# Two head mixes of an attention block pair, moved into the four 64x64 quadrants of TensorE

## The chip, the cores and the metric

The kernel runs on one NeuronCore of one Trainium2 chip. Its engines are TensorE (PE: matrix products into PSUM; a separate instruction, shown as PEld, loads the stationary operand), VectorE (DVE), ScalarE (ACT), GpSimd (POOL) and SyncE (SP), whose queue issues every transfer between device memory and SBUF. Each engine works through its own instructions in program order and waits on semaphores where it needs another engine's result. The metric is the device time of one execution in microseconds. Before the change it was 1627.17 us, the median of three runs.

## The reference

Attention whose heads are mixed twice, followed by a gated two-layer product, all in float32. Eight batches, 12 heads, 448 positions, head size 64; the second part has width 768 and hidden width 1024.

```python
scores = scale * np.matmul(q, k.transpose(0, 1, 3, 2))       # 8 x 12 x 448 x 448
scores = np.einsum('bhij,hg->bgij', scores, w_pre)           # first head mix, 12 x 12
scores = scores - np.max(scores, axis=-1, keepdims=True)
attn = np.exp(scores)
attn = attn / (np.sum(attn, axis=-1, keepdims=True) + 1e-09)
attn = np.einsum('bhij,hg->bgij', attn, w_post)              # second head mix, 12 x 12
attn_out = np.matmul(attn, v)
a = x @ w1                                                   # x: attn_out as 3584 x 768
b = x @ w2
h = a * b @ w3
out = h @ w_out
```

## The kernel before, in words

The scores of a batch are computed head by head (`qk`, lines 196 and 197) and stored to device memory, so that they can be read back with another layout: rows of (position, head). A **block** is `IB` = 10 query positions of one batch with all 12 heads, that is 120 rows of 448 scores. A batch has `NB` = 45 blocks, the last of them 8 positions wide; there are 360 blocks in all.

For each block:

- `fetch` (line 212) reads the 120 rows from device memory, four blocks ahead of their use.
- `mix` (line 233) multiplies them by a 120x120 matrix that has `w_pre` ten times on its diagonal. The first `WHOLE` = 20 blocks do this in float32 as it stands (line 238). From then on the rows are split into two float32r parts by `split_r` (VectorE makes the high part on line 229, GpSimd the rest on line 230), and three products of 448 columns are summed (lines 241 to 243). The matrix is scaled by -0.125, so the largest score is the smallest entry.
- `largest` (line 249) takes each row's minimum on VectorE; `exp` (line 256) is the exponential on ScalarE, with the row's sum.
- `scale` makes one over the sum (lines 265 and 266) and multiplies the 120x120 matrix of `w_post` by it, row by row: on VectorE for the first `ACT_W` = 50 blocks (line 270), on ScalarE from then on (line 272).
- `post` (line 274) multiplies four pieces of 112 keys of the exponentials (the stationary operand) by that matrix (line 279). The result has keys on the partitions; line 285 copies it from PSUM to a tile `mt`, which collects `GB` = 15 blocks.

A float32 product appears in the profile as two passes of TensorE, a float32r one as a single pass. After 15 blocks, `av` multiplies `mt` by `v` for each pair of heads (line 310), in two column halves of 64. `qk_first` (line 160) computes the first batch's scores in float32 from two row halves of 64.

Between these steps TensorE works on the second part, called the background: first a folding of `w3` and `w_out` into one matrix (line 368), then the experts of batches 0 and 1 one by one (lines 530 and 561), then those of two batches at a time with seven products in place of eight (line 710). For the folding and the first experts, weights arrive as raw words and are converted in `to_f32` (lines 113 to 117), whose scratch tile `ca` lies in PSUM bank 5.

The order is written out by hand in `run`: one step per block. A step issues, in this order, its transfers, the conversions, the minimum of its block, the scaling of the block before, the next batch's scores, half of the background's share, the post-mix of two blocks earlier, the `av` work if any is due, the other half of the background, the pre-mix of the next block, the copies out of PSUM (`do_ends`) and, from block 20 on, the exponential. The planner `shares` spreads the background so that every step has the same number of passes, with costs of 2 for a piece of scores and 5.4 for an `av`. Copies and sums out of PSUM are held in lists (`ends`, `soon`, `later`) and issued at fixed places, or when `bank` wants a PSUM bank that is still to be emptied.

PSUM has eight banks. Banks 0 and 1 hold scores, 2 and 3 the pre-mix (by turns), 4 the post-mix, 5 the `av` sums and the converter's scratch, 6 and 7 the background. Once two batches are done at a time, the expert groups and the `av` sums take 5, 6 and 7 by turns (`next_bank`, line 599).

```python
for n in range(N + 6):
    ...
    if n < N:
        self.largest(n)
    ...
    if 0 <= n - 1 < N:
        self.scale(n - 1)
    ...
    advance(now // 2)
    if 0 <= n - 2 < N:
        self.post(n - 2)
    ...
    if n + 1 < N:
        self.mix(n + 1)
    self.do_ends()
```

## Time and profile before

| | |
|---|---|
| median of three runs | 1627.17 us (1625.48 to 1627.89) |
| profiled execution, first to last instruction | 1627.4 us |
| TensorE busy | 1579.8 us, 97% |
| ScalarE, VectorE, GpSimd busy | 1065.4, 1026.1, 1069.8 us |
| transfers | 436.48 MB, 268 GB/s on average |
| first block's minimum, last block's minimum | 23.7 us, 1436.3 us |
| granted TensorE clock | 0.990 of full speed |

The profile is of one execution, and it gives no time for that execution besides its span. A line of a group reads: line of the kernel, engine, operation, output and inputs by the program's names, shapes, count, then busy microseconds and mean nanoseconds of one, then the engine's idle time before them and what ended it. A line of the order in time reads: start, length, engine, line, operation, names, shape, count; consecutive instructions of one kind are merged into one line. On TensorE the lengths overlap, since a pass is shown until its last result is out: what one costs is read from one start to the next. `128*112 128x448` is a product with 128 rows and 112 columns of stationary operand, and 448 columns that move.

### The profile page before, as it was taken

The numbers are of one execution on the slowest core, as the hardware profiler recorded it, in microseconds if no ns is written. First come the engines' busy times: TensorE is split into PE (matmuls) and PEld (weight loads), VectorE is DVE, ScalarE is ACT, GpSimd is POOL, SyncE is SP. The second block draws the span as 40 slices with busy tenths as digits, with TensorE's granted clock in tenths as the row PEclk, the third lists the DMA queues.
The fourth block names the chain that finished last, engine by engine and source line by source line (L and its number), as shares of the span: only waits on it lengthen the run. The fifth ranks groups of instructions, "written<-read, shape, count | busy, mean of one in ns | idle before, by whom it ended". The sixth has DMA issues, their size and how long they took to land. (4 is left out here: it accounts for less than half of the span.)

```text
span 1627.4 us, 32069 instructions
## 1 busy us (share of the span) xinstructions
PE 1579.8 (97%) x10528; PEld 1416.6 (87%) x10528; DVE 1026.1 (63%) x2245; ACT 1065.4 (65%) x2554; POOL 1069.8 (66%) x904
## 2 busy tenths in 40 slices
PE   5999999999999999999999999999999999999999
PEld 2569998888899988988999899999999898999988
DVE  4868668778657877853465465655565567634573
ACT  3878768889867777776776676676775554542321
POOL 1347556667757877975577776877676666655774
PEclk7999999999999999999999999999999999999999
DMA  8989869999899999999988888889888766678875
GB/s 253 339 260 278 246 206 302 296 298 292 261 294 310 311 331 312 298 329 313 280 253 272 265 243 244 249 248 319 277 247 260 227 184 205 207 229 297 281 235 178
DMA packets 233906, 436.48 MB, mean 268 GB/s; under 512 B 21838, under 2 KB 159054, under 8 KB 233678
## 3 DMA queue, kind: packets, MB, share of 16 engines
q1 hardware_dynamic: 233742, 434.44, 84.6%
q8 instruction: 85, 1.39, 0.4%
q14 instruction: 79, 0.65, 0.1%
HBM read 300.27 MB, written 134.09 MB: 267 GB/s over the span
## 5 line engine op out<-in xcount | busy, mean ns | idle before, releaser
L230 POOL TENSOR_TENSOR rl<-r,rh 120x448 fp32r<-120x448 f32 (+1 forms) x340 | 422.9, 1244 | 275.5 <-DVE rh L229 79.8
L249 DVE TENSOR_REDUCE mn<-psm 120x1 f32<-120x448 f32 x360 | 223.9, 622 | 384.2 <-PE psm L243 373.6
L279 PEld LDWEIGHTS pso<-w,e 120*112 120x112 f32 (+1 forms) x2880 | 346.7, 177 | 35.8 <-ACT w L272 16.5
L279 PE MATMUL pso<-w,e 120*112 120x120 f32 (+1 forms) x2880 | 357.6, 267 | 10.9 <-ACT w L272 8.8
L285 ACT COPY mt<-pso 112x480 f32<-112x480 f32 x360 | 205.4, 571 | 199.4 <-PE pso L279 198.0
L710 PE MATMUL e<-eh,wu 128*128 128x448 f32 x1008 | 304.3, 371 | 0.6 <-DVE c L664 0.6
L256 ACT ACTIVATE e<-psm,mn 120x448 f32<-120x448 f32 x360 | 226.7, 630 | 17.8 <-DVE mn L249 17.6
L201 ACT COPY st<-psq 112x448 f32<-112x448 f32 x336 | 175.4, 533 | 56.9 <-PE psq L197 23.4
L229 DVE CAST rh<-r 120x448 fp32r<-120x448 f32 (+1 forms) x340 | 206.7, 608 | 2.5 <-DMA r<-raw_d 1.3
L710 PEld LDWEIGHTS e<-eh,wu 128*128 128x128 f32 x1008 | 187.2, 188 | 15.7 <-DVE c L664 1.4
L710 PE MATMUL e<-el,wu 128*128 128x448 f32 x504 | 187.6, 372 | 2.8 <-POOL el L649 2.8
L186 POOL TENSOR_TENSOR ql<-kq,qh 64x448 fp32r<-64x448 f32 x84 | 99.6, 1186 | 112.1 <-ACT qh L183 89.5
L310 PE MATMUL psa<-mt,v 112*64 112x150 f32 (+1 forms) x2304 | 158.5, 294 | 3.2 <-DMA v<-v 1.8
L310 PEld LDWEIGHTS psa<-mt,v 112*64 112x64 f32 x2304 | 145.1, 138 | 9.7 <-DMA v<-v 2.2
L664 DVE TENSOR_TENSOR c<-c,e 128x448 f32<-128x448 f32 x168 | 101.3, 616 | 67.4 <-PE e L710 62.6
L196 PE MATMUL psq<-kk,qh 128*112 128x448 f32 x336 | 126.0, 375 | 4.4 <-ACT st L201 4.3
L241 PE MATMUL psm<-rh,wph 120*120 120x448 f32 (+1 forms) x340 | 129.7, 381 | 0.0
L530 PE MATMUL eg<-xh,wu 128*128 128x448 f32 x384 | 127.3, 381 | 0.0
L272 ACT ACTIVATE w<-wpo,ri 120x120 f32<-120x120 f32 x310 | 123.0, 397 | 6.3 <-DVE ri L266 5.6
L243 PE MATMUL psm<-rl,wph 120*120 120x448 f32 (+1 forms) x340 | 124.2, 365 | 1.1 <-POOL rl L230 1.1
L242 PE MATMUL psm<-rh,wpl 120*120 120x448 f32 (+1 forms) x340 | 124.2, 365 | 0.0
L197 PE MATMUL psq<-kk,ql 128*112 128x448 f32 x336 | 123.1, 366 | 0.0
(116 smaller groups left out, 2996.6 us busy)
## 6 DMA issues: line engine op xcount, KB each, us to landing
r<-raw_d SPq DMA_DIRECT2D x352, 210.0 KB, 5.1
raw_d<-st SPq DMA_DIRECT2D x168, 392.0 KB, 4.9
wu<-w_d SPq DMA_DIRECT2D x104, 384.0 KB, 5.7
wu<-s_d SPq DMA_DIRECT2D x96, 384.0 KB, 4.3
v<-v SPq DMA_DIRECT2D x144, 224.0 KB, 4.4
wu<-w_d SPq DMA_DIRECT2D x51, 512.0 KB, 6.2
kq<-kq SPq DMA_DIRECT2D x42, 448.0 KB, 6.2
wu<-s_d SPq DMA_DIRECT2D x36, 512.0 KB, 4.4
```

What stands on the lines that cost most here:

```text
L196: nc.tensor.matmul(p, qh[:, cols], kk, start=True, stop=False)
L201: copy(st[:, c % 2], p)
L229: nc.vector.tensor_copy(rh[:K], r[:K])
L230: nc.gpsimd.tensor_tensor(rl[:K], r[:K], rh[:K].bitcast(F32), op=ALU.subtract)
L241: nc.tensor.matmul(p[:K, :S], self.wph[:K, :K], rh[:K], start=True, stop=False)
L249: nc.vector.tensor_reduce(mn[:K], p[:K, :S], axis=AX.X, op=ALU.min)
L256: nc.scalar.activation(e[:K], p[:K, :S], AF.Exp, bias=mn[:K], scale=-1.0, accum_out=sm[:K])
L279: nc.tensor.matmul(p[:, j, :, :w], e[:K, j * JT:(j + 1) * JT], w2[:K, :, :w], start=True, stop=True)
L285: self.ends.append((4, lambda: copy(dst, p[:, :, :, :w])))
L310: nc.tensor.matmul(self.psa[rows, g % 3, :W], v[:, j, rows], mt[:, j, 2 * g + s, :W], start=(j == 0), stop=(j == NJ - 1))
L530: nc.tensor.matmul(p, u[:, k % (K1 // 2), x], xs[y][:, k], start=(k == 0 and t == 0), stop=(k == K1 - 1 and t == 2))
L710: nc.tensor.matmul(p, w[:, k, x], ops[m, k][y], start=(k == 0 and t == 0), stop=(k == nk - 1 and t == 2))
```

## The change

Blocks are handled two at a time, 180 **sets** of two. A block's 10 positions are cut into two halves of `IH` = 5, so 60 rows (`HK`) of (position, head); one half is laid at partition 0, the other at partition 64 (`PP`). `fetch` reads both blocks of a set with two transfers, on even steps.

- **Pre-mix**: four float32 products, unsplit, one for each half (row quadrant, by `s`) and block (column quadrant, by `c`). A half's two blocks go to one PSUM bank, 2 or 3. The splits (`split_r`) and the three-part product are gone.
- **Minimum, exponential, scaling**: two instructions of each per set, one per half, on 128 partitions that hold both blocks. The scaling matrix has 60 columns instead of 120 and is always made on VectorE.
- **Post-mix**: for each half, seven pieces of 64 keys and each block, one float32 product with 60 moving columns: 28 per set. The block sets the row quadrant and the PSUM bank (4 or 5), the piece's parity sets the column quadrant. `put` copies one block per instruction to `mt`, which now has 128 partitions; `v` is padded to match.
- **Order**: an even step issues the minima at its start and the exponentials at its end; the odd step after it the scaling at its start, and at its end the post-mix followed directly by the next set's pre-mix. `av` goes ahead of the background, in odd steps only. The planner counts 8.6 passes for the mixes of an odd step.
- **Banks**: the experts take banks 6 and 7 by turns instead of 5, 6 and 7; the `av` sums share bank 2 with the pre-mix; the converter's scratch tile `a` lies in SBUF.

The diff, cut to its core (a line of "..." where lines are left out; the functions as they were stand above):

```diff
@@ -23,12 +23,15 @@
 KF, K1 = FF // 128, DM // 128
-WHOLE = 20
+IH = IB // 2
+HK = H * IH
+PP = 64
+JB = S // PP
+SETS = NB * B // 2
 FIRST = 48
 LATE = 2 * NB + GB + 2
-ACT_W = NB + 5
 PAIRS = ((0, 0), (0, 1), (1, 0))
@@ -109,7 +112,7 @@
-        a = self.bank(5, f"ca{name}").bitcast(I32)[:, :n]
+        a = self.cx.tile([128, CW], I32, tag="a", name=f"ca{name}", bufs=1)[:, :n]
         nc.vector.tensor_scalar(a, top, 3, 0x3FFFFFFF, op0=ALU.logical_shift_left, op1=ALU.bitwise_and)
@@ -209,80 +212,90 @@
     def width(self, n):
         return min(IB, S - n % NB * IB)
...
+    def fetch(self, m):
+        r = self.rp.tile([128, 2, S], F32, tag="r", name=f"r{m}", bufs=3)
+        self.rs[m] = r
+        b, t = divmod(2 * m, NB)
+        if t + 1 < NB and self.width(2 * m + 1) == IB:
+            src = self.raw_d[b][t * IB:(t + 2) * IB].rearrange("(c s i) h j -> s (i h) c j", c=2, s=2)
+            for s in range(2):
+                self.nc.sync.dma_start(r[s * PP:s * PP + HK], src[s])
+            return
+        for c in range(2):
+            b, t = divmod(2 * m + c, NB)
+            for s in range(2):
+                k = self.half(2 * m + c, s)
+                src = self.raw_d[b][t * IB + s * IH:t * IB + s * IH + k].rearrange("i h j -> (i h) j")
+                self.nc.sync.dma_start(r[s * PP:s * PP + H * k, c], src)
+
+    def half(self, n, s):
+        return min(IH, self.width(n) - s * IH)
+
+    def mix(self, m):
+        nc, r = self.nc, self.rs.pop(m)
+        ps = [self.bank(2 + s, f"psm{m}_{s}") for s in range(2)]
+        for c in range(2):
+            for s in range(2):
+                k = slice(s * PP, s * PP + H * self.half(2 * m + c, s))
+                nc.tensor.matmul(ps[s][c * PP:(c + 1) * PP, :S], self.wsc[k], r[k, c], start=True, stop=True)
+        self.psm[m] = ps
+
+    def largest(self, m):
+
+        nc, mns = self.nc, []
+        for s in range(2):
+            mn = self.ep.tile([128, 1], F32, tag="mn", name=f"mn{m}_{s}", bufs=4)
+            nc.vector.tensor_reduce(mn, self.psm[m][s][:, :S], axis=AX.X, op=ALU.min)
+            mns.append(mn)
+        self.mns[m] = mns
+
+    def exp(self, m):
+        nc, self.es[m] = self.nc, []
+        for s, (p, mn) in enumerate(zip(self.psm.pop(m), self.mns.pop(m))):
+            e = self.ep.tile([128, S], F32, tag="e", name=f"e{m}_{s}", bufs=4)
+            sm = self.ep.tile([128, 1], F32, tag="sm", name=f"sm{m}_{s}", bufs=4)
+            nc.scalar.activation(e, p[:, :S], AF.Exp, bias=mn, scale=-1.0, accum_out=sm)
+            self.es[m].append((e, sm))
+
+    def scale(self, m):
+        nc, self.w2s[m] = self.nc, []
+        for s, (e, sm) in enumerate(self.es[m]):
+            sa = self.ep.tile([128, 1], F32, tag="sa", name=f"sa{m}_{s}", bufs=2)
+            ri = self.ep.tile([128, 1], F32, tag="ri", name=f"ri{m}_{s}", bufs=2)
+            w2 = self.ep.tile([128, HK], F32, tag="w2", name=f"w2{m}_{s}", bufs=4)
+            nc.vector.tensor_scalar_add(sa, sm, 1e-9)
+            nc.vector.reciprocal(ri, sa)
+            nc.vector.tensor_scalar_mul(w2, self.wpo, ri)
+            self.w2s[m].append(w2)
+
+    def post(self, m):
+        nc, w2s = self.nc, self.w2s.pop(m)
+        if any(b in (4, 5) for b, _ in self.ends):
+            self.do_ends()
+        for s, ((e, _), w2) in enumerate(zip(self.es.pop(m), w2s)):
+            for j in range(JB):
+                a, z = divmod(j, 2)
+                at = (2 * a + s) * HK
+                for c in range(2):
+                    k = slice(c * PP, c * PP + HK)
+                    nc.tensor.matmul(self.pso[c][z * PP:(z + 1) * PP, at:at + HK], e[k, j * PP:(j + 1) * PP], w2[k],
+                                     start=True, stop=True)
+        for c in range(2):
+            n = 2 * m + c
+            w, (b, t) = self.width(n), divmod(n, NB)
+            a, u = divmod(t, GB)
+            if u == 0:
+                self.mt[b, a] = self.mp.tile([128, NJ, H, GB * IB], F32, tag="mt", name=f"mt{b}_{a}")
+            src = self.pso[c][:, :NJ * 2 * HK].rearrange("p (j s g i) -> p j s g i", j=NJ, s=2, g=H)
+            dst = self.mt[b, a][:, :, :, u * IB:u * IB + w]
+            self.ends.append((4 + c, lambda dst=dst, src=src, w=w: self.put(dst, src, w)))
+
+    def put(self, dst, src, w):
+        if w == IB:
+            self.nc.scalar.copy(dst.rearrange("p j g (s i) -> p j s g i", s=2), src)
         else:
...
+            for s, k in ((0, IH), (1, w - IH)):
+                self.nc.scalar.copy(dst[:, :, :, s * IH:s * IH + k], src[:, :, s, :, :k])
@@ -301,8 +314,7 @@
         if g % 3 == 0:
-            self.i_psa = self.next_bank() if self.pairs else 5
-            self.psa = self.bank(self.i_psa, f"psa{b}_{a}_{g}")[:, :3 * GB * IB].rearrange("p (g i) -> p g i", g=3)
+            self.psa = self.bank(2, f"psa{b}_{a}_{g}")[:, :3 * GB * IB].rearrange("p (g i) -> p g i", g=3)
         v, mt = self.vs.pop((b, a, g)), self.mt[b, a]
@@ -321,15 +333,15 @@
-            self.ends.append((self.i_psa, leave))
+            self.ends.append((2, leave))
         elif g % 3 == 2:
             q = self.psa[:, :, :W]
-            self.ends.append((5, lambda: nc.scalar.copy(h, q)))
-            self.soon.append((5, lambda: nc.vector.tensor_tensor(l, q, h.bitcast(F32), op=ALU.subtract)))
+            self.ends.append((2, lambda: nc.scalar.copy(h, q)))
+            self.soon.append((2, lambda: nc.vector.tensor_tensor(l, q, h.bitcast(F32), op=ALU.subtract)))
         self.later.append(self.load_v)
@@ -598,7 +610,7 @@
         self.n_groups += 1
-        return 5 + self.n_groups % 3
+        return 6 + self.n_groups % 2
@@ -784,10 +796,13 @@
         self.sz = self.sz.rearrange("p j g i -> p (j g i)")[:, :H * S].rearrange("p (h j) -> p h j", h=H)
-        w = self.kp.tile([128, S], F32R, tag="qh", name="wpre_s").bitcast(F32)[:GI, :GI]
-        self.wsc = cp.tile([GI, GI], F32, name="wsc")
+        w = self.kp.tile([128, S], F32R, tag="qh", name="wpre_s").bitcast(F32)[:, :PP]
+        self.wsc = cp.tile([128, PP], F32, name="wsc")
         nc.sync.dma_start(w, self.wpre)
-        self.wpo = cp.tile([GI, GI], F32, name="wpo")
+        self.wpo = cp.tile([128, HK], F32, name="wpo")
+        self.pso = [self.ps.tile([128, 512], F32, tag=f"b{4 + c}", name=f"pso{c}") for c in range(2)]
+        for p in self.pso:
+            nc.vector.memset(p[PP:, (NJ - 1) * 2 * HK:NJ * 2 * HK], 0.0)
         nc.sync.dma_start(self.wpo, self.wpost)
@@ -832,7 +843,8 @@
                 for g in range(HP):
-                    avs.setdefault(b * NB + (a + 1) * GB + (2 if g < 3 else 5), []).append((b, a, g))
+                    n = (b * NB + (a + 1) * GB + 2) | 1
+                    avs.setdefault(n if g < 3 else n + 2, []).append((b, a, g))
@@ -844,7 +856,7 @@
-            other = [len(qks.get(n, [])) * 2 + len(avs.get(n, [])) * 5.4 for n in range(first, last)]
+            other = [len(qks.get(n, [])) * 2 + len(avs.get(n, [])) * 5.4 + n % 2 * 8.6 for n in range(first, last)]
             level = (sum(other) + count) / (last - first)
@@ -882,18 +894,15 @@
         others(1)
-        for n in range(LF - 1):
-            self.fetch(n)
+        for m in range(LF // 2):
+            self.fetch(m)
         next(fold_pieces)
         next(fold_pieces)
-        self.split_r(0)
         self.mix(0)
-        self.fetch(LF - 1)
         others(2)
-        self.split_r(1)
@@ -936,8 +945,9 @@
                 next(setup, None)
-            if LF <= n + LF < N:
-                self.fetch(n + LF)
+            m, odd = divmod(n, 2)
+            if not odd and LF <= n + LF < N:
+                self.fetch(m + LF // 2)
             self.do_later()
@@ -957,16 +967,11 @@
                 self.split_kq(*x, nc.gpsimd, nc.gpsimd)
-            if n < N:
-                self.largest(n)
-            if n < WHOLE:
-                self.exp(n)
-
-
-            if 0 <= n - 1 < N:
-                self.scale(n - 1)
-            if n + 2 < N:
-                self.split_r(n + 2)
+            if m < SETS:
+                if odd:
+                    self.scale(m)
+                else:
+                    self.largest(m)
             self.do_soon()
@@ -993,22 +998,20 @@
+            for x in avs.get(n, []):
+                self.av(*x)
             advance(now // 2)
-            if 0 <= n - 2 < N:
-                self.post(n - 2)
+            self.do_ends()
             for x in firsts.get(n, [])[1:]:
                 self.later.append(self.qk_first(*x, (next(turn), next(turn))))
-            for x in avs.get(n, []):
-                self.av(*x)
             advance(now - now // 2)
-            if n + 1 < N:
-                self.mix(n + 1)
+            if odd and m < SETS:
+                self.post(m)
+                if m + 1 < SETS:
+                    self.mix(m + 1)
             self.do_ends()
-            while self.last:
-                self.last.pop()()
-
-            if WHOLE <= n < N:
-                self.exp(n)
+            if not odd and m < SETS:
+                self.exp(m)
             if third:
```

91 lines of the change are left out of this document (13 added, 78 removed).

## The prediction

> **What bounds the kernel now.** I read the page first, then the busy time by stage, then the head mixes in order of time on TensorE, then the other engines' groups.
>
> ```profile
> span 1627.4 us, 32069 instructions
> PE 1579.8 (97%) x10528; PEld 1416.6 (87%) x10528; DVE 1026.1 (63%) x2245; ACT 1065.4 (65%) x2554; POOL 1069.8 (66%) x904
> DMA  8989869999899999999988888889888766678875
> ```
>
> ```profile
> 24.00:248.00 224.00, 213.34 (x1318) 173.17 (x1317) 158.73 (x396) 164.41 (x383) 109.15 (x101) 0.96 0.86 269
> 248.00:753.00 505.00, 493.45 (x3526) 447.21 (x3525) 367.46 (x785) 396.40 (x969) 368.79 (x302) 1.00 0.93 304
> 753.00:1440.00 687.00, 679.41 (x4698) 625.28 (x4697) 396.66 (x914) 450.44 (x1099) 475.56 (x400) 1.00 0.81 248
> 1440.00:1627.40 187.40, 183.12 (x966) 166.94 (x964) 92.77 (x130) 47.42 (x94) 113.21 (x94) 1.00 0.77 252
> ```
>
> ```profile
> 24.00:248.00 224.00, 30.15 (x49) 34.96 (x96) 0.96 0.86 269
> 248.00:753.00 505.00, 85.59 (x138) 99.39 (x276) 1.00 0.93 304
> 753.00:1440.00 687.00, 107.81 (x173) 124.72 (x348) 1.00 0.81 248
> ```
>
> The second fence is busy time by stage (PE, weight loads, DVE, ACT, POOL, clock, DMA share, GB/s); the third is the same stages for the tile of row minima alone (DVE, ACT, then as before), so its DVE count is the number of blocks. TensorE is busy in 95 to 99% of the three stages with mixes while no other engine passes 79%. A microsecond taken from TensorE's own stream therefore shortens the span, until something else is late. The DMA share of 0.93 between 248 and 753 is the nearest other limit. The last 187.4 us hold expert work alone and the change does not touch them. Two blocks, the unit of the change, now take 2 x 505/138 = 7.32 us in the middle stage and 2 x 687/173 = 7.94 us in the long one. The span, 1627.4, and the median of the timed runs, 1627.17, differ by 0.2 us, so sums against the one stand for the other.
>
> **What a block's mixes cost TensorE now.** A stretch of the long stage, on PE in order of time (start, length, instruction):
>
> ```profile
> 900.62 0.98 PE L279 MATMUL pso<-w,e 120*112 120x120 f32 x8
> 901.37 0.45 PE L710 MATMUL e<-el,wu 128*128 128x448 f32 x1
> 901.65 0.56 PE L710 MATMUL e<-eh,wu 128*128 128x448 f32 x2
> ...
> 902.45 0.37 PE L241 MATMUL psm<-rh,wph 96*96 96x448 f32 x1
> ...
> 903.06 0.36 PE L196 MATMUL psq<-kk,qh 128*112 128x448 f32 x1
> ```
>
> Lengths overlap, so I go from start to start. A float32 product is two passes: four products of the post-mix stand as x8. From their start to the next pass's are 901.37 - 900.62 = 0.75 us, and the pass behind them holds TensorE 0.28 instead of the 0.20 that L241 to L196 show per pass ((903.06 - 902.45)/3), so 0.83. The pre-mix's three split passes take 0.61. One block: 1.44; two blocks: 2.88 us.
>
> **What it will cost: several tiles at once.** The trace has no product in a 64x64 tile, but products in half-array tiles, on the column side and on the row side:
>
> ```profile
> 866.50 0.98 PE L279 MATMUL pso<-w,e 120*112 120x120 f32 x8
> 867.41 3.28 PE L310 MATMUL psa<-mt,v 112*64 112x150 f32 x48
> 870.62 0.47 PE L241 MATMUL psm<-rh,wph 120*120 120x448 f32 x1
> 870.93 0.37 PE L242 MATMUL psm<-rh,wpl 120*120 120x448 f32 x1
> ```
>
> ```profile
> 39.97 0.92 PE L238 MATMUL psm<-r,wsc 120*120 120x448 f32 x2
> 40.82 1.01 PE L160 MATMUL psz<-kqz 64*112 64x448 f32 x4
> 41.76 0.44 PE L368 MATMUL psf<-fo,fw 128*128 128x384 f32 x1
> ```
>
> ```profile
> L279 PE MATMUL pso<-w,e 120*112 120x120 f32 (+1 forms) x2880 | 357.6, 267 | 10.9 <-ACT w L272 8.8 <-ACT mt L285 2.0
> ```
>
> Columns: 48 passes of 150 take 3.21 us, 0.067 each. The post-mix's spacing follows from its row of 0.98 and its pass of 267 ns (the group just above): seven spacings are 0.71, 0.102 each, 0.85 ns a column; its eight are 0.82. One at a time, 150 columns would take 0.128, so two run side by side. Rows: four passes of 448 take 0.94, while L238 takes 0.85 for two that cannot share. Again two at once. Nothing shows four at once; both splits together is what the change needs. I take four, because rows and columns each pair up fully, and keep two as the other bound.
>
> **Pass price in a tile.** A post-mix pass now moves 60 columns (0.051 us at 0.85 ns) against weights of 64. The weight loads give a second bound:
>
> ```profile
> L279 PEld LDWEIGHTS pso<-w,e 120*112 120x112 f32 (+1 forms) x2880 | 346.7, 177 | 35.8 <-ACT w L272 16.5 <-ACT mt L285 4.5 <-ACT e L256 1.3
> L310 PEld LDWEIGHTS psa<-mt,v 112*64 112x64 f32 x2304 | 145.1, 138 | 9.7 <-DMA v<-v 2.2 <-DVE cx L117 1.9 <-issue 0.6
> ```
>
> 48 weight columns less are 39 ns less, so 64 columns stream in about 64 x 0.81 = 52 ns. I take 0.053 a pass. Two blocks now have 2 x 7 x 2 = 28 products, 56 passes. Column tile 0 has j = 0, 2, 4, 6 of both sets, so the fuller tiles have 8 products: 16 passes, **0.85 us**. Pre-mix: four products of 448, one per tile, two passes of 0.38: **0.76**. **Changing the tiling:** post-mix before L310 lasts 0.91 instead of 0.82 (0.09), L310 lasts 3.21 where 24 pairs at 150 x 0.85 ns are 3.06 (0.15), the pass after takes 0.31 instead of 0.20 (0.11): **0.35** a visit. Post-mix and next pre-mix stand together, so one visit per two blocks. The sum is 1.96 against 2.88: 0.92 us less, times 180 is 166. The first 20 blocks now use the unsplit form, 0.85 instead of 0.61: 5 more. 1627 - 171 = **1456** with nothing waiting.
>
> A row of the trace has 0.067 us between starts in a row of passes; the change asks for one pass each 0.053/4 = 0.013. The Trainium skill (TensorE: Matmul & The Clock Gate, "Wait — 56ns, not 53.3ns?") says that start-to-start never goes below about 25 ns however narrow the product, and that instruction decode can cost about 62 ns a matmul. By 25 ns the post-mix would be 56 x 0.025 = 1.4 us, an estimate from that page, and the whole about 1555 before waits; no row here has passes dense enough to show such a floor.
>
> **The other engines.**
>
> ```profile
> L249 DVE TENSOR_REDUCE mn<-psm 120x1 f32<-120x448 f32 x360 | 223.9, 622 | 384.2 <-PE psm L243 373.6 <-PE psm L238 9.4
> L256 ACT ACTIVATE e<-psm,mn 120x448 f32<-120x448 f32 x360 | 226.7, 630 | 17.8 <-DVE mn L249 17.6
> L256 ACT ACTIVATION_READ_ACCUMULATOR e<-psm,mn 120x1 f32 x360 | 72.2, 201 | 0.0
> L285 ACT COPY mt<-pso 112x480 f32<-112x480 f32 x360 | 205.4, 571 | 199.4 <-PE pso L279 198.0
> L272 ACT ACTIVATE w<-wpo,ri 120x120 f32<-120x120 f32 x310 | 123.0, 397 | 6.3 <-DVE ri L266 5.6
> L265 DVE TENSOR_SCALAR sa<-sm 120x1 f32<-120x1 f32 x360 | 52.4, 146 | 23.0 <-ACT e L256 20.9
> L266 DVE RECIPROCAL ri<-sa 120x1 f32<-120x1 f32 x360 | 59.1, 164 | 12.3
> L270 DVE TENSOR_SCALAR w<-wpo,ri 120x120 f32<-120x120 f32 (+1 forms) x50 | 21.4, 429 | 1.7
> L229 DVE CAST rh<-r 120x448 fp32r<-120x448 f32 (+1 forms) x340 | 206.7, 608 | 2.5 <-DMA r<-raw_d 1.3 <-POOL wu L123 0.3 <-issue 0.3
> L230 POOL TENSOR_TENSOR rl<-r,rh 120x448 fp32r<-120x448 f32 (+1 forms) x340 | 422.9, 1244 | 275.5 <-DVE rh L229 79.8
> ```
>
> The splits disappear: DVE 207, POOL 423 us, both off the path. ACT loses 123 of scaling; DVE takes it for half as many columns, between 0 and 0.43 us, 0.25 taken: 78 more, under the 207. Minima, exponentials and copies out stay at 360, a few partitions taller at the same length. So no engine rises. Reads of raw scores stay at 360 transfers of the same rows; two per even step for two blocks, issued four blocks ahead as before. V tiles grow by 128/112. The memsets run once at the start, beside the 24 us before the first block.
>
> **The converted weights' scratch tile moves from PSUM to SBUF**, so three of its four VectorE operations read two SBUF tensors.
>
> ```profile
> L629 DVE TENSOR_TENSOR x<-t,x 128x448 f32<-128x448 f32 x18 | 20.4, 1144 | 0.0
> L664 DVE TENSOR_TENSOR c<-c,e 128x448 f32<-128x448 f32 x168 | 101.3, 616 | 67.4 <-PE e L710 62.6 <-issue 3.3 <-POOL c L691 0.7
> ```
>
> Two SBUF sources took 1.14 us, one PSUM source 0.62. That is 0 to 0.5 us on 72 x 3 operations; at the upper end 108 us of DVE, about what the casts return, so I take nothing. The Trainium skill (SBUF — State Buffer, "Who interferes with whom") says an instruction with two SBUF inputs contends with GpSimd reading SBUF. The two rows agree; with POOL losing 423 us the upper end is the less likely by that rule.
>
> **What is late next.** Before, two steps lay between a pre-mix and its post-mix; now it is one even step and the front of an odd one. With 0.92 off, two blocks last 6.40 us in the middle stage and 7.02 in the long one; less the 1.96 of mixes, 4.44 and 5.06 are left from the pre-mix's end to the post-mix's start. In them: the first minimum, 0.62. ACT has two copies out (1.14, begun when the post-mix ended 0.76 earlier, so done at 0.4) and the even step's share of its other work. Per two blocks ACT now has 2 x 396.4/138 = 5.74 in the middle stage; less 2 x 0.40 scaling, 1.66 exponentials and 1.14 copies, 2.14 are left, of which I put 60% into the even step: exponentials from 1.7 to 3.4. Two scalings of (0.15 + 0.16 + 0.25), the second behind the second exponential with 0.15 of handing over: 4.1. Long stage: 2 x 450.4/173 = 5.21, 1.61 left, 1.0 in the even step: 3.1, then 3.8. The second set's weights are wanted 0.43 after the start, at 4.87 and 5.49. It fits with 0.8 and 1.7 us spare. I charge misses: of 69 middle pairs a third late by 0.8 (18 us), of 86 long ones a tenth by 0.7 (6). Behind a late scaling stand post-mix, the next pre-mix and the next block's scores; behind that the next minimum. 1456 + 24 = **1480 us**.
>
> Edits with no charge: the expert groups on two banks instead of three (a group's nine passes last 1.8 us and its sum, 0.62, may be read out during the next; if DVE is more than 1.2 us late TensorE waits), and the attention-times-V sums sharing a pre-mix bank (three 16-pass groups there last 3.2 us, far longer than the copy that frees the bank; if the exponential is late, they wait with it).
>
> **Rivals.**
> - **The chain is the new wait (0.16).** If an ACT copy that waits for the even step's last expert group stands ahead of the exponentials, they start at 3.9 (even end 3.2, 0.2 to hand over, 0.53 copy): weights at 6.3, 1.4 us late in the middle stage, 1.0 in the long one. In half the pairs this is about 92 us: **1550**. For it: ACT is strictly ordered and the exponential is last in its step. Against: few groups leave by an ACT copy. In every pair it is 183: **1639**, slower (0.04).
> - **Short passes run two at a time, long ones four (0.09).** 28 x 0.053 = 1.48 instead of 0.85: 113 us more, and most waits vanish: **1575**. For it: the densest row has 0.067 between starts. Against: that row is full with two.
> - **Only two tiles at once (0.07).** Post-mix 1.48, pre-mix 1.52, switch 0.35 make 3.35 a pair, 0.47 over 2.88: 85 us, less 5 for the first blocks: **1707**, slower; it decides as soon as a pair's mixes pass 2.88. It is also the change not doing what it says.
> - **Transfers bind (0.07).** If 0.93 x 505 = 470 us of transfer time in the middle stage cannot shrink, 441 becomes 470: 1480 + 28 = **1508**. For it: the digits of 9 in the row of DMA shares. Against: TensorE is 98% busy there.
> - **No wait at all, and part of the 48 us in which PE is idle is saved too (0.05):** **1430**.
>
> **How the numbers follow.** Forecast 0.52: 1480, its own range 1445 to 1525. The range 1430 to 1590 takes in the first form of the chain, short passes by twos and the transfers, and leaves out the two slower cases and the edges, some 0.2. About 0.2%, or 3 us, is what this measurement tells from no change. Slower: 0.07 + 0.04 = 0.11; same 0.02 for a chain that eats just the gain; faster 0.87.
>
> **What would show it.** Right: post-mix and pre-mix rows of two blocks within 1.9 to 2.1 us from first start to the next other pass, with four starts of 64x64 passes some 10 ns apart; PE idle ahead of the post-mix under 40 us in all, with DVE's scaling named. Wrong: post-mix over 1.8 us a pair (tiles not side by side); PE waiting on the scaled weights for more than 90 us (chain); expert passes waiting on weight tiles in the middle stage (transfers); passes waiting on DVE sums (two banks).

## The result, and the profile after

The changed kernel takes **1585.53 us** (median of four, 1576.18 to 1591.93) beside 1626.82 for the kernel before on the same chip: a ratio of 0.9737, interval 0.9701 to 0.9774. It is faster, by 41 us; 147 were forecast. The time lies inside the stated range of 1430 to 1590 us, close to its upper end, with little more than a quarter of the gain that the sum gave. The page of the profiled execution begins:

```profile
span 1585.1 us, 45760 instructions
PE 1449.0 (91%) x18108; PEld 1144.7 (72%) x18108; DVE 978.4 (62%) x2215; ACT 990.2 (62%) x2252; POOL 653.4 (41%) x564
```

TensorE's busy time fell by 131 us (1579.8 to 1449.0), the span by 42. So the work went, and some 90 us came back as time in which TensorE stands.

A visit (post-mix and pre-mix of two blocks) in the long stage, on PE in order of time:

```profile
786.67 0.37 PE L722 MATMUL e<-eh,wu 128*128 128x448 f32 x1
786.97 1.09 PE L281 MATMUL pso<-w,e 60*64 60x60 f32 x54
787.85 0.59 PE L240 MATMUL psm<-r,wsc 60*64 60x448 f32 x2
787.89 0.22 PE L281 MATMUL pso<-w,e 60*64 60x60 f32 x2
787.95 0.92 PE L240 MATMUL psm<-r,wsc 60*64 60x448 f32 x6
788.80 0.46 PE L199 MATMUL psq<-kk,qh 128*112 128x448 f32 x1
789.10 0.37 PE L200 MATMUL psq<-kk,ql 128*112 128x448 f32 x1
```

From start to start the 56 passes of the post-mix take 787.85 - 786.97 = 0.88 us and the eight of the pre-mix 788.80 - 787.85 = 0.95. The pass ahead of the visit and the one behind it hold TensorE 0.30 each instead of 0.20. Together 0.88 + 0.95 + 0.10 + 0.10 = 2.03 us, where 1.96 was forecast. One pass each 0.88 / 56 = 0.0157 us is only possible with all four tiles at once: two at a time would need 28 x 0.053 = 1.48 by the prediction's price of a pass. The fuller tiles have 16 passes, 0.88 / 16 = 0.055 each, beside the 0.053 that the prediction took.

The stages after, cut at the row minima of blocks 0, 20, 50, 106, 120, 186, 270 and 358 (busy time by stage for the tile of row minima: stretch, length, DVE, ACT, granted clock, DMA share, GB/s); the rows of blocks 50 to 106 and 120 to 186:

```profile
248.10:460.00 211.90, 32.24 (x56) 37.51 (x112) 0.92 0.87 273
...
509.40:753.40 244.00, 38.06 (x67) 44.44 (x132) 0.99 0.99 331
```

The same cut through the kernel before and four of the experiments below gives the table (us). The forecast's column takes 0.92 off for each pair of blocks and 5 more off for the first twenty, whose unsplit pre-mix cost more before, and has no waits.

| blocks | before | forecast, no waits | after | E1 | E8 | E9 | E10 |
|---|---|---|---|---|---|---|---|
| 0-20 | 91.9 | 77.7 | 94.1 | 92.9 | 94.4 | 88.9 | 84.5 |
| 20-50 | 134.7 | 120.9 | 130.9 | 131.2 | 130.0 | 124.8 | 124.5 |
| 50-106 | 196.9 | 171.1 | 211.9 | 200.0 | 199.8 | 188.1 | 186.9 |
| 106-120 | 51.7 | 45.3 | 49.4 | 46.2 | 45.1 | 45.1 | 46.3 |
| 120-186 | 251.8 | 221.4 | 244.0 | 246.8 | 221.8 | 222.5 | 221.3 |
| 186-270 | 343.1 | 304.5 | 318.2 | 313.0 | 312.9 | 313.3 | 312.6 |
| 270-358 | 339.0 | 298.5 | 316.6 | 304.9 | 309.9 | 304.9 | 303.4 |

Three different things are seen. From block 186 on, 47 of 79 us came. In blocks 120 to 186 only 8 of 30 came, at a DMA share of 0.99. In the first 106 blocks nothing came: 436.9 us after against 423.5 before, where the forecast's column has 369.7, and blocks 50 to 106 alone became 15 us longer. There the granted clock is 0.92, against 1.00 in the same blocks of the kernel before (the first row; the second is blocks 120 to 186 of that kernel, whose DMA share was 0.96 already):

```profile
250.30:447.20 196.90, 34.76 (x56) 40.64 (x113) 1.00 0.92 291
...
498.90:750.70 251.80, 40.84 (x66) 46.80 (x131) 0.99 0.96 321
```

What TensorE waits for, in the whole changed kernel (us in total, times, longest):

```profile
PE pso L281 <- DVE sa L266: 52.3, 46, 4.3
PE pso L281 <- DVE w L268: 14.3, 31, 0.9
...
PE psa L322 <- DMA v<-v: 10.9, 8, 3.2
...
PE psa L322 <- ACT e L257: 7.4, 11, 1.5
...
PE psq L199 <- ACT st L204: 3.7, 1, 3.7
PE psm L240 <- DVE xl L344: 2.6, 12, 0.2
```

The post-mix waits 66.6 us for VectorE's scaling. The largest part, 27.9 us (25.8 and 2.1), lies between 248.1 and 460 us, in blocks 50 to 106; 15.2 (8.3 and 6.9) lie in blocks 186 to 358. How it comes about shows in two late visits. The first is of blocks 50 to 106 (VectorE's rows from the weight conversions to the first set's scaling, one of GpSimd, and the first exponential's sum):

```profile
310.52 1.16 POOL L190 TENSOR_TENSOR kk<-kq,kk 64x448 fp32r<-64x448 f32 x1
310.70 1.40 DVE L117 SCALAR_TENSOR_TENSOR ca<-cs,ca 128x384 int32<-128x384 int32 x1
...
311.71 0.20 ACT L257 ACTIVATION_READ_ACCUMULATOR e<-psm,mn 128x1 f32 x1
...
312.13 0.56 DVE L118 SCALAR_TENSOR_TENSOR ca<-cs,ca 128x384 int32<-128x384 int32 x1
...
312.83 0.56 DVE L120 SCALAR_TENSOR_TENSOR cx<-cm,ca 128x384 f32<-128x384 f32 x1
...
313.30 0.61 DVE L552 TENSOR_TENSOR em<-ea,eg 128x448 f32<-128x448 f32 x1
...
313.83 0.14 DVE L266 TENSOR_SCALAR sa<-sm 128x1 f32<-128x1 f32 x1
```

The sum is there at 311.91; VectorE is in a conversion, takes two more of its operations and one of the experts', and starts the scaling at 313.83, 1.9 us later. TensorE stands 2.53 us ahead of this post-mix. The second late visit is of the long stage (the timeline's rows of DVE and GpSimd, the sums of the exponentials, and the post-mix; reciprocals and the like left out):

```profile
1096.42 1.15 DVE L248 TENSOR_REDUCE mn<-psm 128x1 f32<-128x448 f32 x2 [4.91 <-PE psm L240]
...
1097.49 2.89 DVE L641 TENSOR_TENSOR t1o<-c,t1o 128x448 f32<-128x448 f32 x2
...
1099.22 0.20 ACT L257 ACTIVATION_READ_ACCUMULATOR e<-psm,mn 128x1 f32 x1
...
1099.83 0.21 ACT L257 ACTIVATION_READ_ACCUMULATOR e<-psm,mn 128x1 f32 x1
1100.30 0.61 DVE L676 TENSOR_TENSOR c1o<-c1o,e1o 128x448 f32<-128x448 f32 x1
1100.63 2.23 POOL L661 TENSOR_TENSOR el1o<-t1o,eh1o 128x448 fp32r<-128x448 f32 x2 [0.73 <-ACT eh1o L660]
1100.84 0.14 DVE L266 TENSOR_SCALAR sa<-sm 128x1 f32<-128x1 f32 x1
1101.21 0.61 DVE L268 TENSOR_SCALAR w<-wpo,ri 128x60 f32<-128x60 f32 x1
1101.97 0.68 PE L281 MATMUL pso<-w,e 60*64 60x60 f32 x28 [0.74 <-DVE sa L266]
1102.12 0.80 DVE L268 TENSOR_SCALAR w<-wpo,ri 128x60 f32<-128x60 f32 x1
1103.06 0.68 PE L281 MATMUL pso<-w,e 60*64 60x60 f32 x28 [0.41 <-DVE w L268]
```

The first exponential's sum is there at 1099.42 and the second's at 1100.04. VectorE is in the middle of two expert sums (L641) and takes one more (L676), so its scaling starts at 1100.84, 1.4 us after the first sum. Then the two scalings take 0.61 and 0.80 beside GpSimd's L661. TensorE stands 0.74 us ahead of the first set and 0.41 ahead of the second. From the pre-mix's end at 1096.42 the second exponential is done after 3.6 us and the second scaling after 6.5. Over all visits (worked out from the same rows, medians) it is 3.2 and 4.9; the forecast had 3.1 to 3.4 and 3.8 to 4.1. In the 54 visits in which TensorE stood ahead of the first pass it is 4.1 and 5.7, so there the exponentials are late too.

Two groups of the changed kernel that the forecast had priced:

```profile
L268 DVE TENSOR_SCALAR w<-wpo,ri 128x60 f32<-128x60 f32 x360 | 159.5, 443 | 12.6
L117 DVE SCALAR_TENSOR_TENSOR ca<-cs,ca 128x384 int32<-128x384 int32 x64 | 49.4, 772 | 2.2
```

The scaling's shortest, median and longest time in ns:

```profile
L268 DVE TENSOR_SCALAR w<-wpo,ri x360: 251/253/1334, 28.6 to 1392.3; 128x60 f32<-128x60 f32 x180
```

Taken at 0.25 us, it took that in the median, but 0.443 in the mean and up to 1.33. The mean is a mixture: the 199 scalings with no GpSimd operation beside them took 0.251 to 0.257 us, the 161 others 0.77 in the median (worked out from the rows of both engines). The conversion's L117 took 0.772 in the mean; before, the same operation stood at 0.562 (L114 of the kernel before, shown with the scratch experiment). It is a mixture too: 0.56 in the median with GpSimd idle, 1.37 beside a GpSimd operation.

### The profile page after: what moved, and what is told of

The parts are those of the page before. It is cut to its first block, busy times and chain, and to the rows that moved or that the text cites. A ratio compares the mean times of both kernels' runs of the same rounds, so it can differ in the third digit from the quotient of the medians.

```text
span 1585.1 us, 45760 instructions
## 1 busy us (share of the span) xinstructions
PE 1449.0 (91%) x18108; PEld 1144.7 (72%) x18108; DVE 978.4 (62%) x2215; ACT 990.2 (62%) x2252; POOL 653.4 (41%) x564
## 4 chain that ended last, share of the span: by engine, by line
PE 62%; DVE 16%; DMA 11%; ACT 7%; issue 3%; SPq 1%; POOL 0%; DVEq 0%; ACTq 0%; POOLq 0%
PE e L722 16%; PE psa L322 9%; PE pso L281 9%; PE psm L240 7%; DVE w L268 4%; DMA raw_d<-st 4%; PE psq L199 3%; PE e3o L722 3%; DMA v<-v 3%; PE e2o L722 3%; PE eg L542 3%; PE e1o L722 2%; PE psf L380 2%; ACT e L257 2%; PE psq L200 2%
## 5 line engine op out<-in xcount | busy, mean ns | idle before, releaser
L248 DVE TENSOR_REDUCE mn<-psm 128x1 f32<-128x448 f32 x360 | 207.6, 618 | 296.3 <-PE psm L240 295.9
L295 ACT COPY mt<-pso 128x480 f32<-128x480 f32 x352 | 198.0, 621 | 183.8 <-PE pso L281 183.3
L281 PEld LDWEIGHTS pso<-w,e 60*64 60x64 f32 x10080 | 199.7, 138 | 132.4 <-issue 32.5
L281 PE MATMUL pso<-w,e 60*64 60x60 f32 x10080 | 227.8, 228 | 73.3 <-DVE sa L266 52.3
L257 ACT ACTIVATE e<-psm,mn 128x448 f32<-128x448 f32 x360 | 226.0, 638 | 9.4 <-DVE mn L248 9.1
L240 PE MATMUL psm<-r,wsc 60*64 60x448 f32 (+1 forms) x1440 | 195.5, 580 | 11.3 <-DMA r<-raw_d 8.7
L322 PE MATMUL psa<-mt,v 128*64 128x150 f32 (+1 forms) x2304 | 160.4, 296 | 20.3 <-DMA v<-v 10.9
L322 PEld LDWEIGHTS psa<-mt,v 128*64 128x64 f32 x2304 | 147.2, 139 | 37.1 <-ACT e L257 18.0
L268 DVE TENSOR_SCALAR w<-wpo,ri 128x60 f32<-128x60 f32 x360 | 159.5, 443 | 12.6
L676 DVE TENSOR_TENSOR c<-c,e 128x448 f32<-128x448 f32 x168 | 101.3, 616 | 68.7 <-PE e L722 63.6
L661 POOL TENSOR_TENSOR el<-x,eh 128x448 fp32r<-128x448 f32 x90 | 105.9, 1195 | 72.5 <-ACT eh L660 48.0
```

Of the source, the lines that this page charges most:

```text
L240: nc.tensor.matmul(ps[s][c * PP:(c + 1) * PP, :S], self.wsc[k], r[k, c], start=True, stop=True)
L248: nc.vector.tensor_reduce(mn, self.psm[m][s][:, :S], axis=AX.X, op=ALU.min)
L257: nc.scalar.activation(e, p[:, :S], AF.Exp, bias=mn, scale=-1.0, accum_out=sm)
L268: nc.vector.tensor_scalar_mul(w2, self.wpo, ri)
L281: nc.tensor.matmul(self.pso[c][z * PP:(z + 1) * PP, at:at + HK], e[k, j * PP:(j + 1) * PP], w2[k], start=True, stop=True)
L295: self.nc.scalar.copy(dst.rearrange("p j g (s i) -> p j s g i", s=2), src)
```

## The experiments

Each run is named by its edit. E1, E2 and E3 start from the changed kernel, B1 and B2 from the kernel before, the others from an experiment. Times are medians; ratios are to the kernel before, run on the same chip.

### E1: the post-mix one set later

The theory is that late weights (the first rival, "the chain") hold the kernel: with one more set between pre-mix and post-mix, no weight can be late. The rival theory is that transfers hold it.

```
-                    n = (b * NB + (a + 1) * GB + 2) | 1
+                    n = b * NB + (a + 1) * GB
+                    n += 4 if n % 2 else 3
...
-            if odd and m < SETS:
-                self.post(m)
+            if odd:
+                if 0 < m <= SETS:
+                    self.post(m - 1)
```

> The changed kernel, but the post-mix of a set stands one set later (next to the pre-mix two sets ahead), with the attention-times-V work moved behind it. Nothing else differs. Theory CHAIN (the gain was eaten because minimum, exponential and scaling must fit between a pre-mix and the post-mix two steps on): in the trace after, TensorE stands 71 us ahead of post-mixes and 42 us inside them, and 88 us pass at half clock against 34 before, which costs up to 27 us. With 7 us more room all of that goes: 1586 - 113 - 27 = 1446 at the best, 1450 to 1480 expected. Rival TRANSFERS (transfers are 0.98 busy from 450 to 750 us): the middle stage stays at its 300 us and loses only what lies outside, 1475 to 1500. Rival BANKS or SCRATCH (two banks for experts, or the scratch tile in SBUF, took the gain): 1560 or more.

Measured: 1555.71 us (1552.07 to 1560.82), ratio 0.9561 (0.9529 to 0.9592). TensorE's group of the post-mix in E1 (busy and mean, then the idle time ahead of it):

```profile
L281 PE MATMUL pso<-w,e 60*64 60x60 f32 x10080 | 209.2, 225 | 0.0
```

and the waits of PE in E1:

```profile
PE psa L322 <- DMA v<-v: 21.4, 7, 5.6
PE psa L322 <- ACT e L257: 13.8, 13, 2.4
PE psq L199 <- ACT st L204: 12.9, 10, 4.1
...
PE psm L240 <- ACT e L257: 8.3, 7, 2.4
PE psm L240 <- DVE xl L344: 5.5, 12, 3.1
```

The idle time ahead of the post-mix is 0.0, so the lateness is gone entirely, and yet only 30 us came back. The five waits shown stand at 61.9 us where they were 24.6 in the changed kernel (with nothing for the pre-mix on the exponential): 37 of the 66.6 us moved to other places, and 66.6 - 37.3 = 29.3 is about what the span gained. The clock wasn't won back either: the expectation counted 88 us at half clock, and E1 has 94. The measured time meets none of the three expectations. The table says where it didn't help: blocks 120 to 186 (246.8 us) and 0 to 50.

### E2: exponential and scaling ahead of the even step's closing work

If VectorE's order alone makes the weights late, moving the scaling ahead of the closing copies and sums should help as much as E1.

```
-                if odd:
-                    self.scale(m)
-                else:
+                if not odd:
...
-            self.do_ends()
...
+                self.scale(m)
+            self.do_ends()
```

> The changed kernel, but exponential and scaling are both issued ahead of the copies and sums that end the even step; before, the exponentials came after them and the scaling at the start of the odd step, so VectorE reached it behind those sums. In the trace after, the second exponential is done 3.2 us after the pre-mix and the second scaling only at 4.9 (medians), and TensorE is ready at 4.5. Theory CHAIN with VectorE's order as the late link: scaling at about 3.2 + 1.0 = 4.2, most waits go: 1500 to 1535. If the exponential itself is the late link, nothing is gained: 1575 to 1590. If sums pushed behind the scaling then hold up the expert groups: slower than 1590.

Measured: 1581.0 us (1577.32 to 1591.7), ratio 0.9728 (0.968 to 0.9777), which is the changed kernel's. The closing copies and sums are not by themselves what makes the weights late. But the conversions, which an even step issues earlier, are still ahead of the scaling: in blocks 50 to 106 the post-mix of E2 waits 28.0 us for it (26.7 and 1.3), where the changed kernel has 27.9. Whether a scaling ahead of the conversions would be in time is not shown.

### B1: the kernel before with two expert banks

```
-            self.i_psa = self.next_bank() if self.pairs else 5
+            self.i_psa = 5
...
-        return 5 + self.n_groups % 3
+        return 6 + self.n_groups % 2
```

> The kernel before with one part of the change alone: in the last stage expert groups take banks 6 and 7 by turns, and the attention-times-V sums always bank 5. Theory CHAIN: the same within 0.3%, 1623 to 1632. Rival BANKS: the part that ate the gain, so 40 us or more: 1665 and up.

Measured: 1633.46 us, ratio 1.0032 (1.0018 to 1.0046). The third bank is worth some 5 us, so losing it is not the cause of a shortfall of 105.

### B2: the kernel before with the scratch tile in SBUF

```
-        a = self.bank(5, f"ca{name}").bitcast(I32)[:, :n]
+        a = self.cx.tile([128, CW], I32, tag="a", name=f"ca{name}", bufs=1)[:, :n]
```

> The kernel before with one part of the change alone: the converter's scratch tile lies in SBUF instead of PSUM bank 5. In the trace after, three of its operations take 0.66 to 0.77 us instead of 0.54, 42 us of VectorE in all. Theory CHAIN: off the path, the same within 0.3%, 1623 to 1632. Rival SCRATCH: the conversions set the first stage, so most of 42 us come out: 1645 to 1670.

Measured: 1675.89 us, ratio 1.0299 (1.0275 to 1.0324): 48 us slower. The groups by line and shape show the conversion's second operation, in the kernel before:

```profile
L114 DVE SCALAR_TENSOR_TENSOR ca<-cs,ca 128x384 int32<-128x384 int32 x64 | 36.0, 562 | 2.2
```

and in B2:

```profile
L114 DVE SCALAR_TENSOR_TENSOR ca<-cs,ca 128x384 int32<-128x384 int32 x64 | 71.2, 1112 | 2.2
```

Beside the GpSimd splits that the kernel before still has, the operation doubles. In the changed kernel, without the splits, it is 0.772. The Trainium skill (SBUF — State Buffer, "Who interferes with whom") says that a VectorE instruction with two SBUF inputs contends with a GpSimd instruction that reads SBUF; the three rows agree. So do the rows of the first late visit: 1.40 us at 310.70 beside GpSimd, 0.56 at 312.13 without.

### E3: the changed kernel with the scratch tile back in PSUM

Bank 0 is shared with the scores, since no bank is free.

```
-        a = self.cx.tile([128, CW], I32, tag="a", name=f"ca{name}", bufs=1)[:, :n]
+        a = self.bank(0, f"ca{name}").bitcast(I32)[:, :n]
...
-            for x in qks.get(n, []):
-                store = self.qk(*x, nq % 2, nc.scalar.copy)
+            for k, x in enumerate(qks.get(n, [])):
+                store = self.qk(*x, (k + 1 if fold_pieces or unit_pieces else nq) % 2, nc.scalar.copy)
```

> The changed kernel with the converter's scratch tile in PSUM again (bank 0; while weights are converted the scores' pieces start on bank 1). Theory SCRATCH (moving the tile alone cost 48 us in the kernel before, 13 in blocks 0 to 50 and 36 in 50 to 106): a good half of that comes back here, where GpSimd is less busy: 1545 to 1565, all of it in the first 106 blocks. If the cost in the kernel before came from GpSimd's splitting, which the change removes, nothing is gained: 1575 or more.

Measured: 1594.85 us, ratio 0.981 (0.9792 to 0.9828), nothing gained. Blocks 50 to 106 gained 7 us (211.9 to 204.7) and blocks 0 to 20 lost 14 (94.1 to 108.2) to the shared bank.

### E4: E1 and E3 together

The edit is the diffs of E1 and E3.

> The post-mix one set later (as e1_later_post) and the scratch tile in PSUM (as e3_scratch_psum). e1 alone gave 1556: its blocks 0 to 106 took 324 us, as the kernel before (324), though TensorE's own work there fell by some 45. Theory SCRATCH: that is what the first 106 blocks lack; 1510 to 1530. Theory TRANSFERS for the rest: blocks 120 to 186 stay at 240 us or more (247 in e1, 0.99 of the transfer time busy), where TensorE's own work asks for 222.

Measured: 1565.67 us, ratio 0.9633 (0.9614 to 0.9652), 10 more than E1. Its conversion is back at 0.562 us an operation, and blocks 50 to 106 gain only 5 us on E1 (194.8 against 200.0). As far as the shared bank lets it be read, the move to SBUF costs the changed kernel some 5 to 7 us and not B2's 48, so most of B2's price seems to have come from the splits that the change removes. The sharing hides some of it: in blocks 50 to 106 of E4 the scores wait 8.0 us (5.0 and 3.0) for VectorE. The 1510 to 1530 us expected were missed; blocks 120 to 186 stayed above 240, as expected.

### E5: the V tiles kept through a batch

The V tiles are loaded once a batch instead of once a group of blocks; from E4. They take six buffers instead of three, and the first ones are loaded earlier. This asks whether blocks 120 to 186 are held by transfers.

```
-        b, a, g = self.v_list.pop(0)
+        b, g = self.v_list.pop(0)
-        t = self.vp.tile([128, NJ, 128], F32, tag="v", name=f"v{b}_{a}_{g}")
+        t = self.vp.tile([128, NJ, 128], F32, tag="v", name=f"v{b}_{g}")
...
-        v, mt = self.vs.pop((b, a, g)), self.mt[b, a]
+        v, mt = self.vs[b, g], self.mt[b, a]
...
-        self.later.append(self.load_v)
+        if a == NG - 1:
+            self.later.append(self.load_v)
...
-        self.v_list = [(b, a, g) for b in range(B) for a in range(NG) for g in range(HP)]
+        self.v_list = [(b, g) for b in range(B) for g in range(HP)]
```

> As e4_both, but each v tile is loaded once per batch and kept for the three attention-times-V rounds instead of being loaded three times: 96 transfers of 256 KB fewer, 25 of 442 MB (to make room, one output tile of the folding and one work tile fewer). Theory TRANSFERS: blocks 120 to 186 lose 6 to 14 us against e4_both, and the waits on v (20 us in e1) go: 10 to 30 us less than e4_both in all. If transfers are hidden after all: within 5 us of e4_both.

Measured: 1550.85 us (1543.74 to 1553.92), ratio 0.9531 (0.9502 to 0.956). Blocks 120 to 186 went from 243.5 to 222.7 us, which is near the forecast's 221.4. So the V loads held that stage. Blocks 20 to 50 lost 12 us (135.4 to 147.3); why is not shown. E8 loads V otherwise there.

### E6: pre-mix and post-mix apart

Two visits for each pair instead of one, from E4: this prices the change of tiling.

```
+            if odd and m + 1 < SETS:
+                self.mix(m + 1)
...
-            if odd:
-                if 0 < m <= SETS:
-                    self.post(m - 1)
-                if m + 1 < SETS:
-                    self.mix(m + 1)
+            if odd and 0 < m <= SETS:
+                self.post(m - 1)
```

> As e4_both, but the pre-mix stands ahead of the second half of the background instead of right behind the post-mix, so TensorE changes its tiling twice as often. By the forecast's price of 0.35 us a visit: 180 x 0.35 = 63 us more than e4_both where nothing else limits, 40 to 65 with the stages that something else limits. If changing the tiling is nearly free: within 10 us of e4_both.

Measured: 1664.91 us, ratio 1.0244 (1.0225 to 1.0264), 99 more than E4, where 180 x 0.35 is 63. In blocks 270 to 358 it is 18.2 us on 44 pairs, 0.41 each, which is an upper bound: the pre-mix now waits there too, 7.6 us for ScalarE's copy of the `av` sums. The rest lies in the stages before, with new waits. Two mixes on their own, in that stage:

```profile
1303.00 0.37 PE L722 MATMUL e<-el,wu 128*128 128x448 f32 x1
1303.30 0.98 PE L240 MATMUL psm<-r,wsc 60*64 60x448 f32 x8
1304.21 0.67 PE L722 MATMUL e<-eh,wu 128*128 128x448 f32 x2
1304.72 0.36 PE L722 MATMUL e<-el,wu 128*128 128x448 f32 x1
1305.01 1.15 PE L281 MATMUL pso<-w,e 60*64 60x60 f32 x56
1306.09 0.67 PE L722 MATMUL e<-eh,wu 128*128 128x448 f32 x2
```

On entry the pass ahead holds TensorE 0.30 (0.10 more); on leaving the two passes at 1304.21 hold it 0.51 instead of 0.41. The pre-mix alone is 1304.21 - 1303.30 = 0.91 us, the post-mix alone 1306.09 - 1305.01 = 1.08. With 0.10 on either side of each, the two are 2.39, against 2.03 together: a visit more costs 0.36 us without any wait, which is the forecast's 0.35.

### E7: two of the four conversion operations left out

From E1; asks whether VectorE's conversions hold the first 106 blocks.

```
-        nc.vector.scalar_tensor_tensor(a, top, -0x40000000, a, op0=ALU.bitwise_and, op1=ALU.bitwise_or)
-        nc.vector.scalar_tensor_tensor(a, low, 29, a, op0=ALU.logical_shift_right, op1=ALU.bitwise_or)
```

> As e1_later_post, but two of the converter's four VectorE operations are left out (those that merge the exponent's top bit and the low bits, so the converted weights are wrong; 72 x 1.5 us, 108 us of VectorE by the trace after). Theory VECTOR: blocks 0 to 106 (324 us in e1 as in the kernel before, where TensorE's own work fell by 45) are held by VectorE's conversions and by the minima and exponentials that stand behind them: they fall to 285 to 300, the whole to 1520 to 1535. Rival TRANSFERS (0.82 to 0.92 busy there): the same within 8 us, 1548 or more.

Measured: 1535.91 us (1532.47 to 1536.87), ratio 0.9433 (0.9412 to 0.9454), 20 less than E1. By the cut of the table the first 106 blocks took 405.2 us where E1's took 424.1, 19 less; 369.7 is the forecast's. So the two operations are worth about a third of the 54 us by which E1 is over the forecast there.

### E8: V kept from the second batch on

From E1. From the second batch on V is loaded once a batch, into six buffers instead of three. To make room, the scratch tile shares the converter's output tile in SBUF, and the experts have one work tile fewer.

```
+        x = self.cx.tile([128, CW], F32, tag="x", name=f"cx{name}")[:, :n]
+        a = x.bitcast(I32)
...
-        t = self.vp.tile([128, NJ, 128], F32, tag="v", name=f"v{b}_{a}_{g}")
+        t = (self.vp2 if b and g > 2 else self.vp).tile([128, NJ, 128], F32, tag="v", name=f"v{b}_{a}_{g}")
...
-        v, mt = self.vs.pop((b, a, g)), self.mt[b, a]
+        v, mt = self.vs[b, 0 if b else a, g], self.mt[b, a]
...
-        self.later.append(self.load_v)
+        if b == 0 or a == NG - 1:
+            self.later.append(self.load_v)
```

> As e1_later_post, with v kept for the three rounds of a batch from batch 1 on (loaded once instead of three times), without e5's smaller buffers in the first stage and with the scratch tile in SBUF sharing the converter's output tile. Theory TRANSFERS for blocks 120 to 186 (247 us in e1, 223 in e5): they fall to 220 to 228 and nothing else moves: 1530 to 1540. If e5's gain came from elsewhere: 1550 or more.

Measured: **1534.18 us** (1530.57 to 1536.86), ratio 0.942 (0.9392 to 0.9448). It leaves nothing out and is 51 us under the changed kernel. Blocks 120 to 186 by the same cut, in E1:

```profile
493.70:740.50 246.80, 38.04 (x67) 44.55 (x132) 0.96 0.99 332
```

and in E8:

```profile
492.00:713.80 221.80, 38.00 (x66) 44.59 (x132) 1.00 1.01 341
```

The stage is 25 us shorter with fewer bytes to move, at a share that is still at its top. It meets the forecast's 221.4. In E1 the passes that use V wait 19.1 us for it in this stage, in E8 not at all. E1's bytes there, 332 GB/s x 246.8 us = 81.9 MB, would take 240 us even at E8's 341 GB/s, an estimate from the two rows; that the V buffers also let loads start earlier is not separated from it. Blocks 270 to 358 became 5 us longer.

### E9: E8 with the two conversion operations left out

The edit is E7's on E8. It asks whether the causes add up.

> The kernel that keeps v (e8) with two of the four VectorE operations of each weight conversion left out, as in e7, so the converted weights are not the reference's. It asks whether the causes found so far add up, and what is left of the forecast behind them. If they are independent (late weights, transfers of v, conversions on VectorE): 1534 - 20 = 1514 us, with blocks 0 to 106 at about 405 us (e8: 422, e7: 405) and blocks 120 to 186 at 222. If the conversions' 20 us only uncover the transfers or ScalarE in the first 106 blocks, it is the same 20 there and no more than that, and 370 us (the forecast's price for these blocks) stays out of reach by 35. If they overlap with the transfers of v: 1525 or more.

Measured: 1516.14 us (1510.15 to 1520.71), ratio 0.9325 (0.9296 to 0.9353): 18 less than E8. They add up to 2 us. Blocks 0 to 106 took 401.8 us (E8: 424.2) and blocks 120 to 186 took 222.5. To the forecast's 369.7 for the first 106 blocks 32 us are missing, about the expectation's 35.

### E10: E9 with half of the packed weights' transfers left out

```
+        last = None
...
-                words.append(self.words(jobs[n + 2][0], f"{self.n_words}"))
-                self.n_words += 1
+                src = jobs[n + 2][0]
+                if n % 2 == 0 or last[0] != src.shape:
+                    last = src.shape, self.words(src, f"{self.n_words}")
+                    self.n_words += 1
+                words.append(last[1])
```

> As e9, and every second job of the conversions works on the tile of the job before it and loads none of its own, so half of the packed weights' transfers (some 35 of 384 KB, about 13 MB in the first 106 blocks) are left out; the converted weights are wrong. If transfers hold the first 106 blocks behind the conversions (their share there is 0.88 to 0.95): 15 to 25 us less than e9 in these blocks, about 1490 to 1500 us in all. If what is left there is ScalarE's order (scores' copies and exponentials) or the narrow products' own waits: within 5 us of e9.

Measured: 1504.29 us (1499.31 to 1506.74), ratio 0.9239 (0.921 to 0.9267), 12 less than E9, between the two expectations. Of the profiled difference of 8.3 us, 4.4 lie in the first twenty blocks and 1.5 in blocks 20 to 106. So transfers held a little at the very start and hardly anything behind it, as far as two single executions tell: E9's four lie 10.6 us apart. What TensorE waits for here between 24 and 430 us:

```profile
PE psq L201 <- ACT st L206: 9.6, 9, 4.1
PE psm L242 <- ACT e L259: 5.3, 3, 2.4
PE psa L324 <- ACT e L259: 4.8, 6, 1.5
```

19.7 us of waits on ScalarE's copies of scores and its exponentials are left there. Blocks 20 to 106 are 19.4 us over the forecast's column, and 12.4 of these waits (3.0, 5.3 and 4.1) lie in them. No run took them away, so that cause is argued and stays open.

## Why the prediction was right or wrong

**Right: what the mixes cost.** The visit was put at 1.96 us and is 2.03: post-mix 0.88 (0.85), pre-mix and tiling changes 1.15 (0.76 and 0.35). The 0.35 for the change of tiling is 0.36 by E6's rows. All of this is 180 x 0.07 = 13 us of the shortfall. The two rivals about tiles that don't run four at once, 1575 and 1707 us, are out by the row of 56 passes in 0.88 us. So is the floor of 25 ns that the Trainium skill (TensorE: Matmul & The Clock Gate, "Wait — 56ns, not 53.3ns?") states: the passes of four tiles start 15.7 ns apart. Within one tile they start 0.055 us apart, so a floor for a single tile is not ruled out.

**Right: the long stages, once two waits are gone.** For blocks 120 to 358 the forecast's column has 824.4 us, and E8 takes 844.6. Of the 20 us over it, 119 pairs x 0.07 = 8 are the visit's; the rest is other waits. The forecast's 24 us for late weights would fill the gap as well, but in E8 no weights are late, so that match would be luck.

**Right: no charge for two banks (near enough).** 5 us by B1, where nothing was charged.

**Wrong: the term "what is late next", 24 us.** It is 66.6 us of TensorE standing ahead of the post-mix, between the two signs set for it (under 40 for right, over 90 for the chain). What was mis-sized is the way from the exponential to the scaled weights. The working counted ScalarE's other work (2.14 us a pair in the middle stage) but none of VectorE's; it had 0.15 us of handing over and 0.25 for a scaling. The runs show VectorE still in conversions or in expert sums, 1.9 and 1.4 us late in the two visits shown, and a scaling of 0.443 in the mean, 0.61 and 0.80 beside GpSimd in the second visit, which is over the upper bound of 0.43. This is the first rival in kind (the chain), with VectorE as its last link: in the median of all visits ScalarE's exponentials are done when the forecast had them (3.2 us) and VectorE's scaling is late (4.9); in the visits that wait the exponentials are late as well (4.1, and 5.7 for the scaling). That it was lateness that TensorE waited for is shown by E1. That the closing copies and sums alone make it is refuted by E2; the conversions' part is read from the rows, and no run shows it alone.

**Wrong, and larger: the sentence that a microsecond taken from TensorE's stream shortens the span until something else is late.** It was applied to three stages with one check, the busy shares, and only the weights were looked at as "something else". E1 took the lateness away entirely and returned 30 us of 67. The other 37 became waits on V tiles, exponentials, score copies and sums. The sum also had full clock throughout: the changed kernel stood 88 us at half clock, against 34 before. At half clock at most half of the time is lost, so up to (88 - 34) / 2 = 27 us of the shortfall of 105 are clock, and they overlap with the terms below.

**Wrong: the transfers at no charge.** The rival had 0.07 and 28 us, from a share of 0.93 in the middle stage. E1 left blocks 120 to 186 at 246.8 us, 25 over the forecast, at a share of 0.99; E5 and E8 removed V loads (with more V buffers) and fell to 222.7 and 221.8. So that rival was right in mechanism, with V tiles waiting and not the weight tiles that its sign named. Its size was near by luck: 28 us came from a mean share over 248 to 753 us, and the 25 lie in blocks 120 to 186 alone, where the share was 0.96 before. It held *together* with the chain: two rivals were weighed as alternatives and came true in different stages.

**Wrong: the first 106 blocks.** 54 us were taken off there (423.5 to 369.7). After the change they took 13 more. E1 returned 13, two of the conversions' four operations hold about 20 (E7, E9), half of the packed weights' loads about 6 (E10). The forecast's "so no engine rises" failed in this stage: the splits left VectorE, but the conversions that stayed went from 0.562 to 0.772 us, the scaling came on top, and both are longer beside GpSimd (1.37 against 0.56 and 0.77 against 0.25 in the median). The scratch tile at nothing was wrong as an edit by itself (48 us by B2), and nearly right in this kernel (some 5 to 7 us by E3 and E4).

**The account.** From 1585.5: late weights 30 (E1, 1555.7), V transfers 21 (E8, 1534.2), conversions 18 (E9, 1516.1), half the packed loads 12 (E10, 1504.3). E9 and E10 leave work out, so they price causes and are not kernels to use. To 1480 24 us remain, but 24 of that sum were for late weights, which E10 doesn't have: to the 1456 without waits it is 48. By the table 26 of them lie in the first 106 blocks; 13 in all would be the visit's 0.07, and the waits on ScalarE in blocks 20 to 106 are 12.4. The rest is open. A part of what E9 and E10 gained over E1 is clock: 94 us at half clock in E1, 46 in E10.

## What to carry to other kernels

What is saved on the engine that bounds a kernel is worth, stage by stage, only as much as the next limit there allows: shorten the stage by the forecast, work out what every other share would become (0.96 of transfers in 251.8 us is over 1 in 221), and do so in each stage. Rivals of that kind are not alternatives; they can all come true, each in its own stage, and a wait that is removed comes back at the next place, here more than half of it. Where a consumer moves closer to its producers, count the whole way through a busy in-order engine, or leave a full step between them (E1).
